# The head of a fused cross-attention and gated feed-forward kernel, issued in another order

## The chip, the cores and the metric

The kernel runs on one core of one Trainium2 chip. The metric is the device time of one execution in microseconds (us), the median of several runs; lower is better. A core has five engines with an instruction queue each: PE (TensorE, matrix products; its weight loads are shown as PEld), DVE (VectorE), ACT (ScalarE), POOL (GpSimd) and SP (SyncE, which issues DMA transfers). Each engine has its own list of instructions, in the order in which the program records them, and waits where one needs something that is not there yet.

## The reference

Two stages. The first is an attention in both directions between x (8 batches, 8 heads, 512 rows, 64 wide) and a state (8 batches, 8 heads, 32 rows, 64 wide):

```python
scores = scale * np.matmul(x, state.transpose(0, 1, 3, 2))
a = softmax(scores)                       # over the 32 state rows
xread = np.matmul(a, state)
scores2 = scale * np.matmul(state, x.transpose(0, 1, 3, 2))
a2 = softmax(scores2)                     # over the 512 rows of x
sread = np.matmul(a2, x)
y = np.concatenate([xread, sread], axis=2)    # 8 batches of 544 rows
```

The second puts the heads side by side, which gives 4352 tokens of width 512, and runs a gated feed-forward with 1536 inner channels over them:

```python
gate = 1.0 / (1.0 + np.exp(-(y @ w_gate)))
val = y @ w_val
out = (gate * val) @ w_out
```

## The kernel before, in words

**Stages of one batch b.** x of the batch is brought to bf16 and transposed (xT); S_mm multiplies it with the state, spread out so that two heads share one product (sTd for batches 0 and 1, sTz for the later ones); S_exp is the exponential; n_sum and n_mul divide by the row sums and give ab; aT is ab transposed. The state is multiplied with the two weight matrices ahead of time: sw_visit and sw_wide put state x (w_gate, w_val) into PSUM tiles named swp, and sw_cp copies them to SBUF as SW in bf16. gv_mm(b, f) is then the gate and value product of 128 of the 1536 channels, four matmuls of 128x512: both factors are ready, so xread itself is never formed. gv_th is the tanh on ACT (a sigmoid in other clothes), gv_glu the product of gate and value on DVE, which frees the value bank. The output product of a batch is done by seven half-size products in Strassen's manner (h_mm(k, c) for batch 0, c being the half of the rows); it needs sums of glu (h_sum, tile Sm) and sums of w_out (ht_sum, tile tw from tile wo). rd_mm and rd_fin make sread.

**Order.** There is no scheduler: the program is recorded as it is written. The first part of the body, called the head here (275 calls, lines 562 to 837), is a list written out call by call, in which batches 0 and 1, the weights and the start of batch 2 are interleaved. Behind it, step(b, f) runs for b = 2 to 8 and f = 0 to 11 with rules of its own; the first thing that step(2, 0) issues on PE is the swp tiles of batch 3 (sw_six, lines 286 and 293).

**PSUM.** Eight pools of one bank each are named G0, G1, OU, S0, S1, S2, S3 and AT. Every product names its bank or banks, so a product waits until whoever reads the bank's last content is done with it. The bank names in the list are therefore part of the order.

**Transfers.** x of batch 0 comes in four parts through SP (load_xp, line 87). What is cast to bf16 on the way, or loaded while SP is taken, goes through the queue of POOL: x of batch 1 in two halves (load_xh, line 100), the two weight matrices in slices of 256 or 512 channels (load_w, line 104), later states (load_sb, line 527), x of batch 2 (load_x, line 82), and w_out in three thirds (load_wo, line 107). An issue takes POOL 0.74 to 0.92 us. The framework hands out eight semaphores in turn to the transfers of this queue, so the issue of a transfer also waits until the transfer eight places ahead of it has landed. at_xT_dma (line 140) and aT_dma (line 248) are transposing transfers, issued by SP.

**Other lines that the steps name.** 95: the cast of x of batch 0; 135: copy of xT out of PSUM; 147, 156 and 174: S_mm in its forms; 186 and 188: sum and reciprocal of a quarter (nq_sum); 193: nq_mul; 208, 210 and 227: n_sum and n_mul; 234 and 244: aT and its copy; 265 and 268: rd_mm; 329: sw_cp; 343 and 355: gate/value products, in the head and in step; 364: gv_th; 369: gv_glu; 400: ht_sum; 407: h_sum; 425 and 442: output products; 433: w_add and U4; 517: warm, a product of zeros that no one reads; 540 and 543: the state's transposes; 551: sT_pad.

Of the kernel before, what the change touches and what calls it, by code (L numbers as in the profile page):

```python
# [16 lines left out]
def kernel(  # L17
# [310 lines left out]
    def sw_cp(b, lo, w, e, cp):  # L328
        cp(*sw_left.pop((b, lo, w, e)))  # L329
# [387 lines left out]
    load_wo(1)
    sw_cp(0, 512, 1, 0, vec)
    rd_mm(1, S2)
    sw_cp(1, 512, 0, 1, act)  # L720
    gv_mm(0, 5, G1, OU)
    rd_fin(1)
    gv_th(0, 5)
    gv_mm(0, 7, S1, S3)
    sw_cp(1, 512, 1, 0, vec)
    sw_cp(1, 512, 1, 1, act)
    gv_glu(0, 5)
    nc.gpsimd.memset(xs[:, :, :, D:], 1.0)
    gv_mm(0, 4, S0, G0)
    gv_th(0, 7)  # L730
    gv_glu(0, 7)
    gv_th(0, 4)
    gv_glu(0, 4)
    gv_mm(0, 6, S1, G1)
    cast_x(2, pool, 4, 4)
    load_wo(2)
    gv_th(0, 6)
    sw_wide(2, 1, S3, OU, S0, G0, S2, AT)
    gv_glu(0, 6)
    sw_cp(2, 1, 0, 1, act)  # L740
    sw_cp(2, 1, 0, 0, vec)
    sw_cp(2, 1, 1, 1, vec)
    sw_cp(2, 1, 1, 0, act)
    gv_mm(1, 5, S1, G1)
    gv_th(1, 5)
    gv_glu(1, 5)
    sw_cp(2, 1, 2, 0, act)
    h_sum(0, 1, vec)
    gv_mm(1, 6, OU, S3)
    sw_visit(1, 1280, 256, S1, G0)  # L750
    gv_th(1, 6)
    sw_cp(2, 1, 2, 1, act)
    sw_visit(1, 0, 256, S2, S0)
# [283 lines left out]
```

## Time and profile before

| | |
|---|---|
| median of 3 runs | 213.46 us (213.04 to 213.48) |
| the profiled execution | 213.24 us |
| its span, first to last instruction | 211.5 us |
| mean granted TensorE clock | 0.992 |
| busy: PE, DVE, ACT, POOL | 204.5, 160.7, 129.6, 78.7 us |
| HBM read, written | 18.35 MB, 8.91 MB |

The profile is one execution. "Busy" is the time in which an engine has an instruction under way; rows of a timeline give the start, the time taken, the engine, the line, the operation, the output and input tiles with their shapes, and a count where several follow each other. In brackets stands how long the engine stood idle ahead of it, and whom it waited for. A row that covers several instructions includes the tail of the last, which the start of the next may overlap. A row of the DMA view gives the size of a transfer and the time from issue to landing. All times count from the first instruction of the span.

### The profile page before, as it was taken

The page shows a single profiled execution, that of the slowest core. Times are in us where ns is not written, and L with a number is a line of the kernel's source. Part 1 is how long each engine was busy: PE and PEld are TensorE (multiplying, and loading weights), DVE is VectorE, ACT ScalarE, POOL GpSimd, SP SyncE. Part 2 cuts the span into 40 slices and gives each one's busy share as a digit, 9 for nine tenths or more (in the row PEclk, how much of TensorE's full clock was granted, in tenths as well). Part 3 has the DMA queues.
Part 4 walks back from the last instruction along what each step waited for, and adds up shares of the span by engine and source line. Part 5 has one row for each costly group of instructions (what it writes and reads, how often), then busy time and mean ns, then how long its engine had stood idle before and what let it go on. Part 6 is the DMA issues. An engine that isn't in the chain of part 4 may idle for free.

```text
span 211.5 us, 5331 instructions
## 1 busy us (share of the span) xinstructions
PE 204.5 (97%) x2089; PEld 133.4 (63%) x2089; DVE 160.7 (76%) x308; ACT 129.6 (61%) x244; POOL 78.7 (37%) x104
## 2 busy tenths in 40 slices
PE   7789999999999999999999999999999999999992
PEld 2555443677666666565656565657566666788982
DVE  2698899998987788578876887687848876864682
ACT  3878898754767477855786578647774673233210
POOL 8899467599042705900391029301500000000010
PEclk9799999999999999999999999999999999999999
DMA  6999999761689943985924621264110500130044
GB/s 190 181 192 192 213 289 192 115 215 38 78 219 342 132 94 133 289 73 160 295 58 48 186 87 28 56 101 175 26 34 1 201 2 0 76 126 0 4 171 126
DMA packets 40920, 27.14 MB, mean 128 GB/s; under 512 B 23616, under 2 KB 38720, under 8 KB 40896
## 3 DMA queue, kind: packets, MB, share of 16 engines
q1 hardware_dynamic: 30544, 19.47, 36.9%
q0 software_dynamic: 9920, 7.01, 20.5%
q10 hardware_dynamic: 432, 0.33, 0.7%
q8 instruction: 16, 0.26, 0.5%
q14 instruction: 8, 0.07, 0.1%
HBM read 18.35 MB, written 8.91 MB: 129 GB/s over the span
## 4 chain that ended last, share of the span: by engine, by line
PE 94%; DMA 2%; DVE 1%; ACT 1%; SPq 0%; issue 0%
PE gvp L355 30%; PE outp L425 29%; PE gvp L343 10%; PE gvp L358 5%; PE outp L442 4%; PE swp L286 4%; PE swp L293 2%; PE outp L484 2%; DMA xf<-in_x_dram 2%; PE Sp L147 1%; PE xTp L132 1%; PE outp L467 1%; PE rdp L262 1%; PE warm L517 1%; PE aTp L234 1%; PE rdp L265 1%
## 5 line engine op out<-in xcount | busy, mean ns | idle before, releaser
L369 DVE SCALAR_TENSOR_TENSOR glu<-th,gvp 128x512 bf16<-128x512 f32 (+1 forms) x108 | 70.1, 654 | 36.7 <-PE gvp L355 13.7
L364 ACT ACTIVATE th<-gvp 128x512 f32<-128x512 f32 (+1 forms) x108 | 62.1, 578 | 49.4 <-PE gvp L355 34.8
L355 PE MATMUL gvp<-aT,SW 128*128 128x512 bf16 x288 | 77.5, 380 | 0.1
L329 ACT CAST SW<-swp 128x512 bf16<-128x512 f32 x83 | 46.6, 594 | 9.2 <-PE swp L286 8.3
L425 PEld LDWEIGHTS <-Sm 128*128 128x128 bf16 x324 | 31.7, 98 | 12.6
L355 PEld LDWEIGHTS <-SW 128*128 128x128 bf16 x288 | 26.6, 98 | 17.3 <-issue 3.6
L200 POOL CAST Eb<-E 128x256 bf16<-128x256 f32 x32 | 12.8, 436 | 52.0 <-ACT E L167 52.0
L425 PE MATMUL outp<-tw,Sm 128*128 128x256 bf16 x240 | 31.8, 273 | 0.0
L425 PEld LDWEIGHTS <-glu 128*128 128x128 bf16 x240 | 23.5, 98 | 10.2
L425 PE MATMUL outp<-wo,glu 128*128 128x256 bf16 x168 | 22.9, 273 | 0.0
L343 PE MATMUL gvp<-aT,SW 128*128 128x512 bf16 x96 | 22.6, 380 | 0.0
L509 POOL DMA_DIRECT2D out_dram<-res x1 | 0.6, 612 | 50.3 <-DVE res L433 50.3
L227 POOL TENSOR_TENSOR ab<-E,ri 128x512 bf16<-128x512 f32 x13 | 14.3, 1101 | 11.7 <-DVE ri L210 7.0
L407 DVE TENSOR_TENSOR Sm<-glu 128x768 bf16<-128x768 bf16 (+1 forms) x34 | 18.0, 535 | 0.0
L433 DVE SCALAR_TENSOR_TENSOR res<-outp,U 128x512 f32<-128x512 f32 x22 | 15.0, 685 | 1.2 <-PE outp L442 0.9
L343 PEld LDWEIGHTS <-SW 128*128 128x128 bf16 x96 | 8.7, 98 | 10.5 <-issue 1.9
L116 POOL CAST xb<-xf 128x1024 bf16<-128x1024 f32 x12 | 13.2, 1127 | 1.6 <-DMA xf<-in_x_dram 1.6
L167 ACT ACTIVATE E<-Sp 128x512 f32<-128x512 f32 x14 | 8.4, 599 | 7.1 <-PE Sp L147 5.7
L358 PE MATMUL gvp<-xb,wgv 128*128 128x256 bf16 x96 | 12.6, 273 | 0.0
L425 PE MATMUL outp<-wo,Sm 128*128 128x256 bf16 x84 | 11.5, 273 | 0.0
L358 PEld LDWEIGHTS <-wgv 128*128 128x128 bf16 x96 | 9.3, 98 | 1.4
L251 POOL CAST xs<-xf 128x1024 bf16<-128x1024 f32 x10 | 10.1, 1040 | 0.0
(106 smaller groups left out, 224.9 us busy)
## 6 DMA issues: line engine op xcount, KB each, us to landing
out_dram<-res SPq DMA_DIRECT2D x14, 512.0 KB, 3.2
xf<-in_x_dram SPq DMA_DIRECT2D x5, 1024.0 KB, 7.5
wo<-in_moe_w_out_dram POOLq DMA_DIRECT2D x3, 512.0 KB, 8.2
xf<-in_x_dram SPq DMA_DIRECT2D x4, 256.0 KB, 4.0
wgv<-in_moe_w_gate_dram POOLq DMA_DIRECT2D x4, 256.0 KB, 7.4
wgv<-in_moe_w_val_dram POOLq DMA_DIRECT2D x4, 256.0 KB, 8.8
xf<-in_x_dram POOLq DMA_DIRECT2D x1, 1024.0 KB, 9.2
xf<-in_x_dram POOLq DMA_DIRECT2D x2, 256.0 KB, 6.2
```

The lines of the kernel that those rows point to most:

```text
L116: cp(xbs[b].rearrange("p c h d -> p h c d")[:, lo:lo + n], (xhs if b in xhs else xfs)[b][:, lo:lo + n])
L200: nc.gpsimd.tensor_copy(Ebs[b][:, c], E1s[b][:, c])
L227: (nc.gpsimd if eng is pool else nc.vector).tensor_tensor(half(b, i, abs_), e1, ri.unsqueeze(len(ri.shape)).to_broadcast(e1.shape), ALU.mult)
L329: cp(*sw_left.pop((b, lo, w, e)))
L343: nc.tensor.matmul(ps, SWs[b][:, g, w, fs], aTs[b][:, :, g], start=(g == 0), stop=(g == 1))
L355: nc.tensor.matmul(ps, SWs[b][:, g, w, fs], aTs[b][:, :, g], start=(g == 0), stop=(g == 1))
L358: nc.tensor.matmul(ps, (wg, wv)[w][:, j, fs], held["XS"][:, j], start=(j == 0), stop=(j == 3))
L364: nc.scalar.activation(th, held["gv", b, f][0], AF.Tanh, scale=0.5)
L369: nc.vector.scalar_tensor_tensor(glus[b][:, f], held["th", b, f], 1.0, held["gv", b, f][1], ALU.add, ALU.mult)
L407: eng.tensor_tensor(S_(b, t)[:, i], a, c, op)
L425: nc.tensor.matmul(wps[key][:, c], lhs[:, i, c * 128:(c + 1) * 128], rhs[:, i], start=(first and c == 0 and i == 0), stop=(i == NF // 2 - ...
L433: nc.vector.scalar_tensor_tensor(to, wps[key], 0.5, held["w", name], ALU.mult, ALU.add)
```

## The change

All of it is in the head; what it computes stays as it was. Every call of the old list stands in the new one, at another place, many with another bank, some on another engine. The few lines below carry what the prediction speaks of; the rest of the list is moved in the same manner.

```diff
+    load_xp(0, nc.sync, 4, 2)
+    load_xp(0, nc.sync, 2, 2)
+    zero(sTd, vec)
     make_identity(nc, ident)
-    load_xh(1, 0, 4)
-    nc.vector.memset(ones, 1.0)
-    cast_s(0, vec)
     cast_xp(0, act, 0, 2)
     load_xh(1, 4, 4)
...
+    warm(3, S3)
     xT_mm(0, 1, S3)
...
-    warm(3, G0)
...
-    aT_cp(0, 0, act)
-    sw_cp(0, 256, 2, 0, vec)
+    aT_cp(0, 0, vec)
+    sw_cp(0, 256, 2, 0, act)
...
+    load_x(2, nc.gpsimd)
+    nc.gpsimd.memset(xs[:, :, :, D:], 1.0)
...
+    load_wo(2)
...
+    load_wo(0)
...
+    load_wo(1)
...
+    gv_glu(1, 6)
+    ht_sum(0, vec)
```

Two halves of x of batch 1 change places, the slices of the weights at channel 0 move ahead, and all three state loads (load_sb) now come behind the eight narrow weight transfers, where one of them came behind four. The thirds of w_out come in the order 2, 0, 1.

On ACT, at the first state x weight copies, before (E is S_exp's output; the quarters of batch 0 are the 128x8x32 ones):

```order
L182 ACTIVATE E_177<-Sp 128x8x32 x2
L135 COPY xT<-xTp 128x1024
L167 ACTIVATE E_265<-Sp 128x8x64
L244 COPY aT<-aTp 128x512 x2
L167 ACTIVATE E_265<-Sp 128x8x64
L329 CAST SW<-swp 128x2x256 x2
L364 ACTIVATE th<-gvp 128x512
L329 CAST SW<-swp 128x2x256 x4
```

and after:

```order
L182 ACTIVATE E_197<-Sp 128x8x32 x2
L167 ACTIVATE E_311<-Sp 128x8x64
L135 COPY xT<-xTp 128x1024
L167 ACTIVATE E_311<-Sp 128x8x64
L244 COPY aT<-aTp 128x512
L329 CAST SW<-swp 128x2x256 x4
L364 ACTIVATE th<-gvp 128x512
L329 CAST SW<-swp 128x2x256 x2
L364 ACTIVATE th<-gvp 128x512 x4
```

Half of the aT copy has gone to DVE, and four SW copies stand ahead of the first tanh where two did.

On POOL, from the last weight slice to the casts of x of batch 2, before (tw is the tile that the later states are loaded to, sTz and xs are filled with constants):

```order
L200 CAST Eb<-E_265 128x256 x4
L111 MEMSET sTz 128x2048
L82 DMA xf<-in_x_dram 128x8x256
L107 DMA wo<-in_moe_w_out_dram 128x4x512
L557 COPY sTz<-sTc 64x24x32 x2
L107 DMA wo<-in_moe_w_out_dram 128x4x512
L728 MEMSET xs 128x32x2
L116 CAST xb<-xf 128x4x4x64
L107 DMA wo<-in_moe_w_out_dram 128x4x512
L407 TENSOR_TENSOR Sm<-glu 128x768
L116 CAST xb<-xf 128x4x4x64
```

and after:

```order
L200 CAST Eb<-E_311 128x256 x4
L527 DMA tw<-in_state_dram 128x4x64
L111 MEMSET sTz 128x2048
L82 DMA xf<-in_x_dram 128x8x256
L710 MEMSET xs 128x32x2
L107 DMA wo<-in_moe_w_out_dram 128x4x512 x3
L116 CAST xb<-xf 128x4x4x64 x2
L407 TENSOR_TENSOR Sm<-glu 128x768
L557 COPY sTz<-sTc 64x24x32 x2
```

The three thirds of w_out are issued in one go, and both casts of x of batch 2 follow without anything between them.

On DVE, around the sums of w_out, before (glu are gv_glu's, rs and ri belong to n_sum of batch 2):

```order
L369 SCALAR_TENSOR_TENSOR glu<-th,gvp 128x512 x3
L400 TENSOR_TENSOR tw<-wo 128x1536 x2
L407 TENSOR_TENSOR Sm<-Sm,glu 128x768
L400 TENSOR_TENSOR tw<-wo,tw 128x1536
L369 SCALAR_TENSOR_TENSOR glu<-th,gvp 128x512
L208 TENSOR_REDUCE rs<-E_911 128x16
L210 RECIPROCAL ri<-rs 128x16
L407 TENSOR_TENSOR Sm<-glu,Sm 128x768
```

and after:

```order
L369 SCALAR_TENSOR_TENSOR glu<-th,gvp 128x512 x3
L400 TENSOR_TENSOR tw<-wo 128x1536
L407 TENSOR_TENSOR Sm<-glu 128x768 x2
L400 TENSOR_TENSOR tw<-wo,tw 128x1536
L400 TENSOR_TENSOR tw<-wo 128x1536
L369 SCALAR_TENSOR_TENSOR glu<-th,gvp 128x512
L208 TENSOR_REDUCE rs<-E_885 128x16
L210 RECIPROCAL ri<-rs 128x16
L433 SCALAR_TENSOR_TENSOR res<-outp,V_911 128x2x256
```

ht_sum(0) now follows gv_glu(1, 6) instead of gv_glu(1, 11), with five gv_glu of batch 1 still to come instead of three, and the two h_sum of the sum tile 2 stand behind it.

More of the change, by code (lines that the diff above doesn't have):

```diff
@@ L586 @@
-    sT_pad(1, act)
-    xT_cp(0, 2, act)
+    cast_xp(0, vec, 2, 2)
+    cast_s(0, act)
+    xT_mm(0, 0, S3)
+    cast_xp(0, act, 4, 2)
+    sT_mm(0, S0)
+    nc.vector.memset(ones, 1.0)
+    xT_cp(0, 0, act)
+    load_xh(1, 0, 4)
+    sT_pad(1, vec)
+    sT_pad(0, act)
+    xT_mm(0, 2, G1)
+    load_w(0, 256, 256)
+    xT_cp(0, 2, vec)
+    load_w(1, 256, 256)
+    warm(3, S3)
+    xT_mm(0, 1, S3)
+    nc.scalar.activation(pre[:, 0:1], ones, AF.Exp)
+    load_w(0, 1024, 256)
+    xT_cp(0, 1, vec)
@@ L717 @@
[L717 to L753, printed above, removed]
+    xT_cp(1, 0, act, 2)
+    S_mm(1, 0, G0)
+    S_exp(1, 0)
+    aT_mm(0, S2)
+    aT_cp(0, 0, vec)
+    sw_visit(0, 256, 256, S3, S1)
@@ new lines @@
+    sw_cp(1, 512, 1, 1, vec)
+    rd_mm(1, G0)
+    gv_mm(0, 6, G1, OU)
+    load_wo(2)
+    sw_cp(1, 512, 0, 0, vec)
+    gv_th(0, 6)
+    gv_mm(0, 5, S2, AT)
+    rd_fin(1)
+    sw_cp(1, 512, 0, 1, act)
+    gv_mm(0, 7, G1, S0)
+    gv_th(0, 5)
+    gv_th(0, 7)
+    gv_mm(0, 4, G0, S2)
+    gv_glu(0, 6)
+    gv_glu(0, 5)
+    gv_th(0, 4)
+    load_wo(0)
+    sw_wide(2, 1, S3, S1, AT, G1, G0, OU)
+    gv_glu(0, 7)
+    load_wo(1)
+    sw_cp(2, 1, 1, 0, act)
+    sw_cp(2, 1, 1, 1, act)
+    cast_x(2, pool, 0, 4)
@@ new lines @@
+    sw_cp(2, 1, 0, 1, act)
+    sT_mm(3, S0)
+    gv_glu(0, 4)
+    sw_cp(2, 1, 2, 0, vec)
+    gv_mm(1, 5, S2, AT)
+    gv_th(1, 5)
+    gv_mm(1, 4, G1, G0)
+    sw_cp(2, 1, 0, 0, vec)
+    sT_cp(3, vec)
+    gv_th(1, 4)
+    gv_glu(1, 5)
+    gv_glu(1, 4)
+    cast_x(2, pool, 4, 4)
+    gv_mm(1, 6, S3, S0)
+    gv_th(1, 6)
+    sw_visit(1, 0, 256, G1, AT)
+    h_sum(0, 0, pool)
+    sw_cp(2, 1, 2, 1, act)
+    gv_glu(1, 6)
+    ht_sum(0, vec)
+    sw_visit(1, 1280, 256, S2, S1)
+    h_sum(2, 0, vec)
@@ L769 @@
-    gv_th(1, 11)
-    at_xT_dma(2)
-    gv_mm(1, 10, G0, S1)
-    gv_glu(1, 11)
-    h_mm(1, 0, AT)
-    h_mm(1, 1)
-    ht_sum(0, vec)
-    h_sum(0, 0, pool)
+    S_mm(2, 0, G1)
+    h_mm(1, 0, OU)
+    sw_cp(1, 0, 2, 1, act)
+    ht_sum(2, vec)
+    h_mm(1, 1)
+    gv_mm(1, 10, S0, S1)
+    gv_th(1, 10)
+    h_sum(1, 0, pool)
+    h_mm(2, 0, S3)
+    gv_glu(1, 7)
+    S_mm(2, 1, AT)
+    S_exp(2, 0)
+    h_mm(2, 1)
+    load_x(3, nc.sync)
+    gv_mm(1, 11, G1, G0)
+    gv_mm(1, 0, S2, S0)
+    n_sum(2, 0)
@@ L777 @@
+    w_keep('V1', 1)
+    S_exp(2, 1)
+    gv_th(1, 11)
+    gv_th(1, 0)
+    w_add(2, 'V1', w_res(0, 0)[:, :, lo_])
+    n_sum(2, 1)
+    gv_glu(1, 11)
+    h_sum(1, 1, pool)
+    gv_mm(1, 1, AT, S3)
+    gv_glu(1, 0)
+    n_mul(2, 0, pool)
+    gv_glu(1, 10)
+    h_mm(6, 0)
     h_mm(5, 0, G1)
-    S_mm(2, 0, OU)
     h_mm(5, 1)
-    ht_sum(2, vec)
-    h_sum(1, 0, vec)
-    load_x(3, nc.sync)
-    ht_sum(1, vec)
-    gv_th(1, 10)
-    h_mm(7, 0, S0)
-    gv_glu(1, 10)
-    sw_cp(1, 0, 2, 0, act)
@@ L788 @@
-    h_sum(3, 0, pool)
-    w_keep('V1', 1)
-    h_mm(6, 0)
-    S_exp(2, 0)
-    n_sum(2, 0)
-    n_mul(2, 0, pool)
-    S_mm(2, 1, G0)
-    aT_dma(2, 0)
-    S_exp(2, 1)
-    gv_mm(1, 0, OU, S2)
-    h_sum(3, 1, vec)
-    gv_th(1, 0)
-    h_mm(6, 1)
+    h_mm(6, 1)
+    h_mm(7, 0, S0)
+    gv_th(1, 1)
+    h_sum(3, 0, vec)
+    h_mm(7, 1)
     w_keep('U2', 1)
-    n_sum(2, 1)
+    cast_x(3, pool, 4, 4)
     ht_sum(3, vec)
     n_mul(2, 1, pool)
-    aT_dma(2, 1)
-    h_U4()
-    gv_mm(1, 1, G0, S1)
```

258 lines of the change are left out of this document (115 added, 143 removed).

## The prediction, made before the changed kernel ran

> **What bounds the kernel now.** I read the page first: the engine totals, the 40 slices and the chain that ended last.
>
> ```profile
> PE 204.5 (97%) x2089; PEld 133.4 (63%) x2089; DVE 160.7 (76%) x308; ACT 129.6 (61%) x244; POOL 78.7 (37%) x104
> PE   7789999999999999999999999999999999999992
> PEclk9799999999999999999999999999999999999999
> PE 94%; DMA 2%; DVE 1%; ACT 1%; SPq 0%; issue 0%
> ```
>
> TensorE is busy for 97% of the span and carries 94% of the last chain. Only the first three slices (5.29 us each) and the very last have PE under nine tenths. The change touches only the head, the code ahead of step(2, 0); all later work is PE-bound in the same order, so whatever the head wins or loses reaches the end of the span whole. I therefore ask one thing: when does PE issue the first row of step(2, 0)? The timeline of PE has that row, the first gate/value product, and what PE waited for ahead of it.
>
> ```profile
> 13.14 0.41 PE L293 MATMUL swp<-wgv,tw 64*32 64x512 bf16 x8 [0.20 <-DMA wgv<-in_moe_w_val_dram]
> 14.77 1.04 PE L343 MATMUL gvp<-aT,SW 128*128 128x512 bf16 x4
> 39.80 1.47 PE L442 MATMUL outp<-wo,glu 128*128 128x256 bf16 x12
> 52.77 0.62 PE L286 MATMUL swp<-wgv,sTc 64*32 64x512 bf16 x16
> ```
>
> The head ends at 52.77. The first product starts at 14.77, behind swp tiles that waited for a transfer of w_val. The timeline of POOL and the DMA view of that stretch say when it landed: 5.09 + 7.9 = 13.0.
>
> ```profile
> 5.09 0.76 POOL L104 DMA_DIRECT2D wgv<-in_moe_w_val_dram  x1
> wgv<-in_moe_w_val_dram POOLq DMA_DIRECT2D x1, 256.0 KB, 7.9
> ```
>
> **First part of the change: up to the first product.** The multiset of instructions in the head is the same (11 warm-up matmuls, 24 gate/value pairs, 14 groups of h_mm and so on); a few copies change engines and everything changes place. The two cast transfers that gate the first swp are still third and fourth on the pool's queue, behind the two halves of x of batch 1, so 13.0 stays. What PE has done before gv_mm(0, 3) is the same set before and after. What changes is who delivers ab, aT and SW for it, and these rows price that.
>
> ```profile
> 6.17 0.68 DVE L95 CAST xf<-xf 128x512 bf16<-128x512 f32 x1 [0.81 <-DMA xf<-in_x_dram]
> 6.76 0.41 DVE L135 COPY xT<-xTp 128x512 bf16<-128x512 bf16 x1
> 10.22 0.42 DVE L186 TENSOR_REDUCE rsq<-E 128x8 f32<-128x256 f32 x1
> 10.68 0.20 DVE L188 RECIPROCAL riq<-rsq 128x8 f32<-128x8 f32 x1
> 10.91 0.96 DVE L193 TENSOR_TENSOR ab<-E,riq 128x256 bf16<-128x256 f32 x2
> 12.57 0.69 DVE L208 TENSOR_REDUCE rs<-E 128x16 f32<-128x512 f32 x1
> 13.29 0.25 DVE L210 RECIPROCAL ri<-rs 128x16 f32<-128x16 f32 x1
> 13.61 0.69 DVE L329 CAST SW<-swp 128x512 bf16<-128x512 f32 x1
> 15.90 2.05 ACT L329 CAST SW<-swp 128x512 bf16<-128x512 f32 x4
> ```
>
> After, DVE runs in one piece from the landing of the third part of x at 6.17: cast 0.68, sT_pad (no row on DVE; between the narrow copy's 0.41 and the 0.69 of an f32 bank, L329; I take 0.6), two xT copies 0.82, a second cast 0.68, four sums with reciprocals 2.48, a wide xT copy (at most two narrow ones, I take 0.7), two products 0.96. That is 6.9, and ends at 13.1 with every tail counted, 12.7 where a start overlaps the tail before it; before, it was 10.91 + 0.96 = 11.87. Then a sum with reciprocal (0.94) and the aT copy (0.41) stand ahead on DVE, and ACT takes its aT half and both SW copies of batch 0 one behind the other (2.05 / 4 = 0.51 each), where before DVE did one of them. So aT is whole at about 14.2, the second SW copy ends at 15.2 (bounds 14.8 and 15.6), and the second matmul of gv_mm(0, 3) runs then, where it ran at 14.77 + 0.22 = 15.0. I take +0.3 for the first product, from 0 to +0.6.
>
> **Second part: from there to h_mm(1, 0).** These are the unit prices of PE, from the chain of waits in order of time.
>
> ```profile
> 17.02 3.45 PE gvp L343 x16
> 33.20 0.56 PE swp L286 x16
> 46.74 3.28 PE outp L442 x30
> ```
>
> A gvp matmul is 0.216, a group of eight swp 0.28, an outp matmul 0.109. Before h_mm(1, 0) the old order had run 22 of the 24 gate/value pairs; the new one has run 20, and one S_mm (0.23) more. So PE gets to h_mm(1, 0) at 39.80 - 2 x 0.86 + 0.23 = 38.3, plus the 0.3 above, less what the order wins back of the old stalls. Those are at most 0.8: 14.77 to 52.77 is 38.0, and 96 gvp (20.7), 84 outp (9.2), 128 swp (4.5) and some 2.8 of small products make 37.2. I take 0.3 of it, so 38.3, from 37.8 to 38.6. DVE gets to ht_sum(0), which reads all of wo, when glu(1, 6) is done: PE's gv_mm(1, 6) ends 1.65 (two swp groups of eight, one pair, S_mm) ahead of h_mm(1, 0), th and glu follow with 0.6 each, so at 37.9.
>
> Both need the last third of wo. Here are the issues on POOL and, from the DMA view of those stretches, the times to landing.
>
> ```profile
> 21.70 0.92 POOL L82 DMA_DIRECT2D xf<-in_x_dram  x1
> 22.59 0.78 POOL L107 DMA_DIRECT2D wo<-in_moe_w_out_dram  x1
> 28.38 0.75 POOL L107 DMA_DIRECT2D wo<-in_moe_w_out_dram  x1
> 31.93 0.74 POOL L107 DMA_DIRECT2D wo<-in_moe_w_out_dram  x1
> xf<-in_x_dram POOLq DMA_DIRECT2D x1, 1024.0 KB, 9.2
> wo<-in_moe_w_out_dram POOLq DMA_DIRECT2D x1, 512.0 KB, 10.6
> wo<-in_moe_w_out_dram POOLq DMA_DIRECT2D x1, 512.0 KB, 8.2
> wo<-in_moe_w_out_dram POOLq DMA_DIRECT2D x1, 512.0 KB, 7.0
> ```
>
> x of batch 2 landed at 30.9, the thirds of wo at 33.2, 36.6 and 38.9: one queue that hands over a third every 2.3 to 3.4 us however early it was issued. The last stood 0.9 ahead of its first use at 39.80. After, the bytes ahead of x are the same, the third state load included, and POOL issues all of it early (x at about 23, the thirds by 26), so nothing there holds the queue. The last third lands between 30.9 + 3 x 2.3 = 37.8 and 38.9; I take 38.35. It is now wanted at 37.9 by DVE and 38.3 by PE, so this wait binds, just. It also absorbs the 0.3 of the first part. Queued behind it on DVE are two h_sum, two ht_sum and glu(1, 7), whose bank gv_mm(1, 11) needs.
>
> at_xT_dma(2) moves up too; its four transposes on SP started at 35.99, 1.3 apart. With x cast in one go on POOL (2 x 1.03 behind 30.9) they start at 33.0 and S_mm(2, 0) needs the second at about 37: hidden, by a microsecond. load_x(3) follows them on SP at about 38, in the tail of the last third; that price has no row and lies in the bounds above. The third state load stands ahead of x, so it is in by 30.9, and sT_mm(3) comes 4.5 of PE work ahead of h_mm(1, 0), at 33.8: nothing. The tightest weight is the wide half of w_val:
>
> ```profile
> 17.85 0.79 POOL L104 DMA_DIRECT2D wgv<-in_moe_w_val_dram  x1
> wgv<-in_moe_w_val_dram POOLq DMA_DIRECT2D x1, 512.0 KB, 10.1
> ```
>
> It landed at 27.95, no later after (the same bytes but one state load ahead), and is wanted 9.95 of PE work ahead of h_mm(1, 0), at 28.35: hidden by 0.4, which I count at nothing; without it the loss is that of the wait for wo, which comes later on the same queue.
>
> **Third part: from wo to the end of the head.** DVE's work up to h_sum(3, 1), for which the fourth matmul of h_mm(3, 0) waits, has these rows.
>
> ```profile
> 39.99 1.82 DVE L400 TENSOR_TENSOR tw<-wo 128x1536 bf16<-128x1536 bf16 x2
> 35.85 1.02 DVE L407 TENSOR_TENSOR Sm<-glu 128x768 bf16<-128x768 bf16 x2
> 38.19 1.88 DVE L369 SCALAR_TENSOR_TENSOR glu<-th,gvp 128x512 bf16<-128x512 f32 x3
> 49.40 1.35 DVE L433 SCALAR_TENSOR_TENSOR res<-outp,U 128x512 f32<-128x512 f32 x2 [0.20 <-PE outp L442]
> ```
>
> Four ht_sum at 0.91, four h_sum at 0.51, five glu at 0.63, two n_sum at 0.94, U4 and one w_add at 0.68: 3.6 + 2.0 + 3.1 + 1.9 + 1.4 = 12.0 with tails, 11.4 where starts overlap tails. PE then has 21 outp (2.3) and rd_mm (0.6): 14.3 to 14.9 in all, I take 14.6. PE's own work behind the last third is 84 outp less the two that need it not, 4 pairs, an S_mm, sw_wide and rd_mm: 14.1, hidden behind the DVE chain. The head ends at 38.35 + 14.6 = 52.95 instead of 52.77: **+0.2**. The profiled execution took 213.24, so 213.44 for one like it; it is 0.22 below the median of the runs, 213.46, and against that I forecast 213.7. This kernel's measurement can tell about 0.2% (0.43 us) from no change.
>
> **The rivals.** *A, faster (0.20):* the queue gives wo at 2.3 us a third, or earlier, and the new order leaves PE no gaps. Then the last third is in at 37.8, the chain behind it is 14.3, the head ends at 52.1: -0.6, 212.9. For it: two of three distances in the rows are 2.3. Against: the middle one is 3.4, and DVE has no gap to give. [...]
>
> *B, slower (0.23):* ACT falls behind at the start, and PE's bank waits push the arrival at h_mm(1, 0) past 38.4, from where each 0.1 counts. The place is gv_mm(1, 8): its value half writes bank G0, in which th(1, 3) still reads the gate of gv_mm(1, 3), and th(1, 3) now stands behind the aT half, four SW copies, th(0, 3) and two more SW copies: 13.6 + 0.5 + 2.05 + 0.6 + 1.0 + 0.6 = 18.4, against PE's arrival at 19.1. With ACT late by more than the 0.7 between, PE stops there and again at each later reuse; I price that at 1.0 in all (two times th's 0.6, less the 0.2 to spare): 214.5.
>
> *C, slower (0.10):* the clock closes late. Three windows of the first stretch, with PE's busy time and, third from the end, the granted clock:
>
> ```profile
> 6.00:7.00 1.00, 0.10 (x2) 0.10 (x3) 0.83 (x2) 0.98 (x2) 1.00 (x2) 1.00 1.20 184
> 7.00:8.00 1.00, 0.73 (x17) 0.60 (x17) 0.59 (x2) 0.89 (x4) 1.00 (x2) 0.94 1.18 149
> 8.00:9.00 1.00, 1.00 (x13) 0.83 (x11) 0.84 (x3) 0.71 (x3) 0.78 (x2) 0.50 1.30 160
> ```
>
> The mean over the span, from the view of the cores:
>
> ```profile
> core 0: 211.5 us, clock 0.992
> ```
>
> The clock fell in the window from 7 to 8 and stood at 0.50 in the next, right behind a microsecond in which PE was busy for a tenth. The new order puts warm(3) into that gap, so I expect the clock open there. But from 11 to 15 PE now waits for ab, aT and SW. If it idles there as long as it did from 6 to 7, the clock falls again, just as the bound part begins. One such fall costs what the mean of 0.992 says: 0.008 x 211.5 = 1.7 us of clock, or 3.4 us at a half. Here it would hit products, and only 0.1 of waiting for wo absorbs it: 213.46 + 1.7 - 0.1 = 215.1. It decides at about 0.9 us of idle time in one piece; my walk has 0.3 to 0.5 in each of two. [...]
>
> **How the numbers follow.** Forecast 0.47 (faster 0.04, same 0.34, slower 0.09), A 0.20 (0.16 faster, 0.04 same), B 0.23 (0.07 same, 0.16 slower), C 0.10 slower: faster 0.20, same 0.45, slower 0.35. The range takes A's end, 213.46 - 0.65 = 212.8, and on the other side the late bounds together (38.9 + 14.9 = 53.8, +1.0) with some of B: 214.7. C and the tails of A and B stay out.
>
> **What would show it.** Right: ht_sum(0) on DVE waits for a DMA of wo for up to 1 us near 38; PE's h_mm(3, 0) waits for DVE; the row at 52.77 comes within 0.5 of it; the first gvp starts at 14.8 to 15.3. A: DVE waits for nothing at ht_sum(0) and the row comes at 52.1. B: ACT's th rows of batch 1 end after PE asks for their banks between 18 and 24. C: a granted clock under 1 behind 14.7. The forecast is wrong if wo lands before 37.5, or if the row at the end of the head has moved by over 0.7 without a wait for wo.

## The result and the profile after

| | before | after |
|---|---|---|
| median (range) | 213.29 us (213.04 to 213.48, 4 runs) | 220.23 us (218.27, 219.18, 221.28, 221.44) |
| mean granted clock of these runs | 0.992 (the profiled one) | 0.999, 0.992, 0.977, 0.975, in that order |
| profiled execution, its span | 213.24, 211.5 | 218.27, 216.5 |
| head ends (first L286 row of step(2, 0)) | 52.77 | 57.86 |

The changed kernel is slower: the ratio is 1.0317, with an interval of 1.0226 to 1.0408. The forecast was 213.7 with a range to 214.7. Left out here and below is one later execution of the changed kernel, in which the clock stood at 0.85 throughout, and out of the ratios single runs over 1.5% above the fastest of their kernel. Two things have to be explained: 5 us in the best run, which had the clock open throughout, and 3.2 us between the runs.

On the page of the changed kernel, PE's total, its 40 slices, its granted clock and the chain that ended last:

```profile
PE 205.2 (95%) x2089; PEld 132.5 (61%) x2089; DVE 164.6 (76%) x309; ACT 128.9 (60%) x243; POOL 79.8 (37%) x104
...
PE   7779999859999999999999999999999999999993
...
PEclk9999999999999999999999999999999999999999
...
PE 73%; DVE 9%; DMA 8%; POOL 5%; issue 2%; ACT 0%; SPq 0%; DVEq 0%; POOLq 0%
```

PE is as busy in all as before (205.2 against 204.5), but the eighth and ninth slices, 38 to 49 us, stand at 8 and 5 tenths, and DVE and POOL now carry part of the last chain, where PE had 94% of it. The clock is open in every slice: warm(3) stands in the gap in which it had closed, and in this run it did not close later either.

The timeline of PE has the places that the prediction named:

```profile
15.16 1.31 PE L343 MATMUL gvp<-aT,SW 128*128 128x512 bf16 x4 [1.03 <-ACT SW L329]
39.60 0.29 PE L147 MATMUL Sp<-sTz,xT 128*128 128x64 bf16 x4 [0.58 <-DMA xT<-xb]
40.10 0.29 PE L147 MATMUL Sp<-sTz,xT 128*128 128x64 bf16 x4 [0.21 <-DMA xT<-xb]
40.23 1.47 PE L442 MATMUL outp<-wo,glu 128*128 128x256 bf16 x12
46.84 2.32 PE L343 MATMUL gvp<-aT,SW 128*128 128x512 bf16 x10 [2.30 <-DVE glu L369]
57.86 0.63 PE L286 MATMUL swp<-wgv,sTc 64*32 64x512 bf16 x16
```

The first product starts at 15.16, 0.4 later than before (forecast 0.3). S_mm(2, 0), forecast as hidden, waits for both of its transposes, and h_mm(1, 0) starts at 40.23 instead of 38.35. A wait of 2.30 follows, in which the value half of gv_mm(1, 11) wants a bank that glu(1, 7) has not read yet. From h_mm(1, 0) to the end of the head pass 17.63 us; the forecast had 14.6. The two differences, 1.88 and 3.03, are nearly the whole 5.09 by which the head ends later than before (57.86 against 52.77); the forecast itself had 0.2.

Why glu(1, 7) is late stands on DVE's timeline:

```profile
39.39 1.23 DVE L400 TENSOR_TENSOR tw<-wo 128x1536 bf16<-128x1536 bf16 x1 [0.98 <-DMA wo<-in_moe_w_out_dram]
40.55 3.90 DVE L407 TENSOR_TENSOR Sm<-glu 128x768 bf16<-128x768 bf16 x2
46.11 0.67 DVE L369 SCALAR_TENSOR_TENSOR glu<-th,gvp 128x512 bf16<-128x512 f32 x1
50.81 0.55 DVE L407 TENSOR_TENSOR Sm<-glu,Sm 128x768 bf16<-128x768 bf16 x1
51.28 1.79 DVE L400 TENSOR_TENSOR tw<-wo,tw 128x1536 bf16<-128x1536 bf16 x1
```

The two h_sum at 40.55 take 1.95 each, where the row of before has 0.51. At 50.81 the same operation takes 0.55, and at 51.28 an ht_sum takes 1.79 instead of 0.91. Nothing in the rows waits; the instructions themselves are long. The timeline of POOL at the same places:

```profile
38.18 1.63 POOL L407 TENSOR_TENSOR Sm<-glu 128x768 bf16<-128x768 bf16 x1
39.77 4.26 POOL L407 TENSOR_TENSOR Sm<-Sm,glu 128x768 bf16<-128x768 bf16 x2
50.88 1.37 POOL L116 CAST xb<-xf 128x1024 bf16<-128x1024 f32 x1
52.20 2.16 POOL L200 CAST Eb<-E 128x256 bf16<-128x256 f32 x4
54.31 2.36 POOL L251 CAST xs<-xf 128x1024 bf16<-128x1024 f32 x2
```

POOL does h_sum(1, 0) and (1, 1) at 39.77, in 4.26 (one alone 1.63, the row at 38.18), and a cast beside the long ht_sum. In the old list h_sum(1, 0) was on DVE, and (1, 1) on POOL at another time.

### The profile page after: what moved, and what is told of

Same layout as the page of the kernel before. It is cut to its first block, busy times and chain, and to the rows that moved or that the text cites. A ratio compares the mean times of both kernels' runs of the same rounds, so it can differ in the third digit from the quotient of the medians.

```text
span 216.5 us, 5323 instructions
## 1 busy us (share of the span) xinstructions
PE 205.2 (95%) x2089; PEld 132.5 (61%) x2089; DVE 164.6 (76%) x309; ACT 128.9 (60%) x243; POOL 79.8 (37%) x104
## 4 chain that ended last, share of the span: by engine, by line
PE 73%; DVE 9%; DMA 8%; POOL 5%; issue 2%; ACT 0%; SPq 0%; DVEq 0%; POOLq 0%
PE gvp L355 29%; PE outp L425 28%; DMA wo<-in_moe_w_out_dram 6%; PE gvp L358 5%; PE swp L286 3%; DVE tw L400 2%; PE outp L484 2%; DMA xf<-in_x_dram 2%; DVE glu L369 2%; PE outp L442 1%; POOL wgv L104 1%; DVE Sm L407 1%; PE swp L293 1%; PE Sp L147 1%; PE outp L467 1%
## 5 line engine op out<-in xcount | busy, mean ns | idle before, releaser
L369 DVE SCALAR_TENSOR_TENSOR glu<-th,gvp 128x512 bf16<-128x512 f32 (+1 forms) x108 | 69.6, 653 | 35.7 <-PE gvp L355 13.8
L425 PEld LDWEIGHTS <-Sm 128*128 128x128 bf16 x324 | 31.7, 98 | 12.6
L200 POOL CAST Eb<-E 128x256 bf16<-128x256 f32 x32 | 13.7, 465 | 53.4 <-ACT E L167 53.4
L407 DVE TENSOR_TENSOR Sm<-glu 128x768 bf16<-128x768 bf16 (+1 forms) x34 | 20.9, 618 | 0.0
L227 POOL TENSOR_TENSOR ab<-E,ri 128x512 bf16<-128x512 f32 x13 | 13.6, 1049 | 15.8 <-DVE ri L210 7.4
L343 PEld LDWEIGHTS <-SW 128*128 128x128 bf16 x96 | 8.8, 97 | 14.6 <-issue 4.1
L358 PE MATMUL gvp<-xb,wgv 128*128 128x256 bf16 x96 | 12.6, 273 | 0.0
```

Source lines behind the costliest of these rows:

```text
L200: nc.gpsimd.tensor_copy(Ebs[b][:, c], E1s[b][:, c])
L227: (nc.gpsimd if eng is pool else nc.vector).tensor_tensor(half(b, i, abs_), e1, ri.unsqueeze(len(ri.shape)).to_broadcast(e1.shape), ALU.mult)
L343: nc.tensor.matmul(ps, SWs[b][:, g, w, fs], aTs[b][:, :, g], start=(g == 0), stop=(g == 1))
L358: nc.tensor.matmul(ps, (wg, wv)[w][:, j, fs], held["XS"][:, j], start=(j == 0), stop=(j == 3))
L369: nc.vector.scalar_tensor_tensor(glus[b][:, f], held["th", b, f], 1.0, held["gv", b, f][1], ALU.add, ALU.mult)
L407: eng.tensor_tensor(S_(b, t)[:, i], a, c, op)
```

## The experiments

Times are of one execution, the fastest, with the clock open where nothing else is said; the kernel before took 212.9 in such runs on every chip used (its lowest runs there are 212.92, 212.86, 212.72 and 212.89). Theory P: DVE's sums, which read two tiles of SBUF, stand still while POOL executes an instruction that reads SBUF, and the other way round. Theory M: those rows are long for a reason of their own (the tiles, the memory traffic). Theory K: the rest comes from falls of the clock. Theory Q: the cast queue, with x of batch 2 ahead, sets when wo and the transposes are in.

**1. The sums taken off POOL, a reading and a writing load in their place.**

```diff
 e1, e2, e3:
-    h_sum(1, 0, pool)
+    h_sum(1, 0, vec)
-    h_sum(1, 1, pool)
+    h_sum(1, 1, vec)
 e2 adds on POOL at both places (no one reads scr):
+    nc.gpsimd.tensor_tensor(scr, S_(0, 0)[:, i], A(0, 0, 0)[:, i], ALU.subtract)
 e3 adds instead, three times at each place:
+    nc.gpsimd.memset(scr, 0.0)
```

Both sums on DVE:

> The changed kernel, with h_sum(1, 0) and h_sum(1, 1) on DVE instead of POOL. Theory P (DVE's sums of two SBUF tiles wait while POOL reads SBUF): the two h_sum of tile 2 on DVE, which took 1.99 us each beside POOL's sums, take 0.5 each; the two moved ones add 0.5 each; the head ends at 57.86 - 2.9 + 1.0 = 55.9 or a little under, and a run at full clock takes 216.3 instead of 218.3. Rival M (DVE's sums are slow because x of batch 3 is landing at over 300 GB/s at that time): all sums on DVE in that stretch stay near 2.0, the head ends at 58 or later, 218.5 or more.

With sums on POOL that no one needs (scr is a part of the tile tw that is free at that time):

> As the one with the sums on DVE, and POOL does two sums of the same tiles and size at the old place, into a tile that nobody reads. Theory P: DVE's sums in that stretch wait for POOL again (1.5 to 2.0 us for at least two of them), the head ends at 57.9 to 58.9, a run at full clock takes 218.3 to 219.3. Rival M: POOL's work changes nothing, the result is that of the kernel without it.

With memsets on POOL:

> As before, but POOL fills the unread tile six times (about 0.7 us each) instead of summing: it is as long busy, and only writes. Theory P in the form that only POOL's reads count: no loss against the kernel with the sums on DVE, head end 55.9, 216.3 at full clock. Rival P2 (any POOL instruction blocks DVE there): DVE's sums of 1 to 2 us, 217.3 or more. Rival M: as without it.

Measured: 217.06, 219.99 (lowest, clock 0.992) and 217.26; ratios 1.022 (1.0136 to 1.0304), 1.0347 (1.0262 to 1.0431) and 1.0195 (1.0121 to 1.0269). The profile of the third is one of its longer runs (220.84), whose clock stood at a half from 11.0 to 21.2; the rows below lie behind that. Here are DVE's row for h_sum(2, 0) and (2, 1) in the three, and what POOL did beside it. The sums on DVE, POOL idle beside the first row:

```profile
40.40 1.01 DVE L407 TENSOR_TENSOR Sm<-glu 128x768 bf16<-128x768 bf16 x2
48.83 1.18 DVE L407 TENSOR_TENSOR Sm<-glu,Sm 128x768 bf16<-128x768 bf16 x1
52.20 1.22 DVE L407 TENSOR_TENSOR Sm<-glu,Sm 128x768 bf16<-128x768 bf16 x1
```

POOL reading:

```profile
41.06 3.90 DVE L407 TENSOR_TENSOR Sm<-glu 128x768 bf16<-128x768 bf16 x2
40.28 4.26 POOL L567 TENSOR_TENSOR tw<-Sm,glu 128x768 bf16<-128x768 bf16 x2
```

POOL writing only:

```profile
44.03 1.01 DVE L407 TENSOR_TENSOR Sm<-glu 128x768 bf16<-128x768 bf16 x2
43.23 4.72 POOL L567 MEMSET tw<- 128x768 bf16 x6
```

The same two instructions on the same tiles take 1.01, 3.90 and 1.01. POOL is busy for over four microseconds in both of the last two; only where it reads does DVE stand. P holds and M falls, by these three rows. In e1 the late sums (48.83, 52.20) are still long, since POOL casts beside them, and so it takes 217.06 where 216.3 was forecast.

**2. The clock behind the wait of 2.30.**

```diff
+    warm(8, S2)
     gv_mm(1, 11, G1, G0)
```

> The changed kernel with eight more warm-up products (8 x 0.216 = 1.73 us at full clock) ahead of gv_mm(1, 11), where PE waits 2.9 us in two pieces. Theory K (the spread from 218.3 to 221.4 and the mean clocks from 0.999 to 0.975 come from a clock that falls behind this wait in some runs): all runs within 1 us of 218.3, mean clock 0.99 or more. Rival: the clock falls elsewhere, and the runs spread by 2 to 3 us as they did, with clocks down to 0.975.

Measured: 218.36, 218.38, 219.53 and 221.17, ratio 1.0265 (1.0189 to 1.034). The spread stays, and the best run is no better than the changed kernel's. The profiled run, the longest, lost its time earlier: its clock stands at a half from 13.7 to 20.6. The run of 219.53 has a mean clock of 0.998, so not all of the spread is the clock's. The fall that lengthens the runs is thus not, or not only, behind that wait. It can be there: with POOL reading, PE waited 3.18 ahead of the same product, and the ten gvp behind it took 4.00 instead of 2.32.

**3. POOL's casts given to ACT, and PE's order.**

```diff
 e4, on top of the sums on DVE:
-    cast_x(3, pool, 4, 4)
+    cast_x(3, act, 4, 4)
-    cast_x(3, pool, 0, 4)
+    cast_x(3, act, 0, 4)
-    at_Eb(2)
+    for c in range(4): act(Ebs[2][:, c], E1s[2][:, c])
 cast_xs(3, ...) stands behind step(2, 1)
 e5, on top of e4:
-    S_mm(2, 0, G1)
     h_mm(1, 0, OU)
...
     h_mm(1, 1)
+    S_mm(2, 0, G1)
...
-    h_mm(6, 0)
     h_mm(5, 0, G1)
     h_mm(5, 1)
+    h_mm(6, 0)
```

> Both sums of the run before this one stay on DVE, and POOL is kept from reading SBUF until the head ends: the two casts of x of batch 3 and the casts to Eb go to ACT, the casts to xs move behind step(2, 1). If POOL's reads are what slows DVE's sums, h_sum(3,0), ht_sum(3) and h_sum(3,1) take 0.5, 0.9 and 0.5 us (1.18, 1.15 and 1.22 with the two sums alone moved), DVE is done with h_sum(3,1) at about 51.8 instead of 53.4, the wait of 0.66 on PE ahead of the fourth matmul of h_mm(3,0) goes, and since PE then has no later DVE work to wait for, the head ends at 55.9 instead of 56.5 and the best run takes 216.4 (217.06 there). If those rows were long for a reason of their own (tile, place in PSUM, the clock), they stay over 1.1 and the best run stays at 217.1. ACT gets some 3 us of casts; if it has no such room, sw_wide's copies come late and the time rises above 217.1.

> As the run with POOL kept silent, and two products move on PE: S_mm(2,0) stands behind h_mm(1,1), so that nothing ahead of h_mm(1,0) needs the transposes of x of batch 2, and both halves of h_mm(5) stand ahead of h_mm(6,0), so that it finds h_sum(1,1) done. If the transposes' landing is a cost of its own, h_mm(1,0) starts when the last third of wo is in, at 39.1 instead of 39.9, and with the wait of 0.85 for Sm gone as well the head ends 1.6 earlier than with POOL silent alone, at about 54.2: 214.8 for the best run. If PE is held by wo and by DVE in any case, the wait moves to h_mm(1,0) and the head gains 0.3 at most: 216.1.

Measured: best runs 217.90 and 217.61, ratios 1.0257 (1.0189 to 1.0324) and 1.0233 (1.0167 to 1.0298). The first forecast of 216.4 failed because the edit did not do what it says: POOL waits for nothing at its place in the list, so the casts to xs ran at once, at 47.66, beside the sums. POOL and DVE of that kernel:

```profile
46.67 1.05 POOL L227 TENSOR_TENSOR ab<-E,ri 128x512 bf16<-128x512 f32 x1 [0.35 <-DVE ri L210]
47.66 2.35 POOL L251 CAST xs<-xf 128x1024 bf16<-128x1024 f32 x2
```

```profile
46.98 1.15 DVE L407 TENSOR_TENSOR Sm<-Sm,glu 128x768 bf16<-128x768 bf16 x1
49.25 1.17 DVE L407 TENSOR_TENSOR Sm<-glu,Sm 128x768 bf16<-128x768 bf16 x1
50.35 0.94 DVE L400 TENSOR_TENSOR tw<-wo,tw 128x1536 bf16<-128x1536 bf16 x1
52.41 0.54 DVE L407 TENSOR_TENSOR Sm<-glu,Sm 128x768 bf16<-128x768 bf16 x1
```

Where POOL reads beside them, h_sum(1, 1) and h_sum(3, 0) are long; behind POOL's last cast, ht_sum(3) and h_sum(3, 1) are at their price. That is P again, row by row. The casts on ACT have a cost of their own: rd_mm waited 0.61 for SW copies. Without the wait for the transposes only 0.3 was gained, as the second reading said. In e5's profile PE waits 1.03 and 0.76 for glu instead, but that is a run of 220.00, whose clock had fallen at 12.1; which wait took over in the best run isn't shown.

**4. x of batch 2 on another queue.**

```diff
 e7, in the changed kernel (e8: the same on top of e5):
-    load_x(2, nc.gpsimd)
+    load_x(2, nc.scalar)
```

> The changed kernel with one edit: x of batch 2 is issued by ACT, on a queue that does not cast, at the same place in the list; the three thirds of wo then follow the weights directly on the cast queue. If that queue's own rate sets when wo is in (a third every 2.3 to 3.4 us behind 1 MB of x), wo lands 4 us earlier, at about 35, x no later than 31, ht_sum(0) starts when glu(1,6) is done, at 38.2 instead of 39.4, S_mm(2,0) does not wait, and the best run takes 217.2 (218.27 with x on the cast queue), since the slow sums beside POOL stay. If the 16 engines or the memory set it, wo lands within 1 us of 39 and the time stays at 218.3.

> POOL silent, the two products moved and x of batch 2 on ACT's queue together. If the costs are the slow sums beside POOL, the wait for the transposes and the wait for wo, in that order, then h_mm(1,0) starts at 38.9 and the head ends at about 54.0: 214.6 for the best run, and what is left above 213.0 (the kernel before) is the late arrival of PE, 38.9 against 38.3 by my walk, and the stretch behind it. If something else holds the head back, the best run stays above 216.

Measured: 223.31 and 223.25 at best, at clocks of 0.981 and 0.985 (no run of the eight has it open), ratios 1.0479 (1.0426 to 1.0532) and 1.0506 (1.0434 to 1.0578). ACT reached the issue only at 29.06, 6 us later than POOL did, and the casts and pad of POOL queued behind the landing at 39.0, so that S_mm(2, 0) waited 7.42 for POOL in e7. The clock fell in it and stood at a half from 44.4 to 51.2, so not all of the loss is the wait. As a test of Q it is half a test: with x out of the way, ht_sum(0) found wo there at 38.41, and the last third had landed at 36.6 (24.3 + 12.3), against 39.1 in the changed kernel (25.2 + 13.9). The better test came with the next group.

**5. POOL really held, the other queue again, and warm-up products.**

```diff
 e9: h_sum(1, 0) and (1, 1) on vec, the second behind gv_glu(1, 7), and:
     h_sum(3, 1, vec)
+    pool(pre[:, 1:2], Sm[:, 3, 5, :1])
+    at_Eb(2)
+    cast_x(3, pool, 4, 4)
+    cast_x(3, pool, 0, 4)
 e11: e9, and load_x(2, nc.scalar) behind gv_th(0, 9)
 e10: the changed kernel, and e12: e11, each with
+    warm(2, G0)
     Sq_mm(0, 0, S0)
...
+    warm(2, G0)
     S_mm(1, 1, S3)
...
+    warm(3, G1)
     gv_mm(0, 3, S3, G1)
```

> Both sums of batch 0 on DVE, the second of them now right behind glu(1,7), and POOL held by a copy of one column of h_sum(3,1)'s result: its casts to Eb, of x of batch 3 and to xs all come behind that. (The run called POOL silent did not silence it: the casts to xs ran ahead, beside h_sum(3,0).) If POOL's reads make DVE's sums long, h_sum(1,1), h_sum(3,0), ht_sum(3) and h_sum(3,1) take 0.55, 0.55, 0.95 and 0.55 us, h_sum(3,1) ends at about 51.6 instead of 53.4, PE waits for no Sm, the head ends at 55.0 (56.5 with the two sums alone moved) and the best run takes 215.6 (217.06 there). If DVE's rows shrink and the end stays, another wait takes over, and the rows of PE name it; if they don't shrink, POOL was not the cause.

> As the run with POOL held, and x of batch 2 goes on ACT's queue, issued behind th(0,9), at about 20.5 (29.1 in the run before that tried this queue, where it landed at 39.0, because ACT got there late). If the cast queue's rate sets when wo is in, wo lands at 35 to 36, x at about 31, ht_sum(0) starts at 38.2, h_mm(1,0) at about 39.0, and the best run takes 0.9 less than with POOL held alone: 214.7. If x lands after 33 on this queue too, POOL's casts and pad come late, and the time does not fall.

> The changed kernel with seven more warm-up products, in the three longest gaps of PE before the first gate/value product: two ahead of the first quarter of S, two ahead of S_mm(1,1), three ahead of gv_mm(0,3). The runs of the changed kernel lie between 218.27 (mean clock 0.999) and 221.44 (0.975), and in two disturbed profiles the clock fell at 10.9 and 13.6 for three and two windows of 3.4 us. If idle PE in these gaps lets the clock fall, all runs now show a mean clock of 0.99 or more and lie within 0.6 of the best, which stays at 218.3 (to 218.6, if the products end after the wait they stand in). If the falls come from elsewhere, the spread of 3 us stays.

> The run with POOL held and x of batch 2 on ACT's queue, with the seven warm-up products as well: the best run as without them (214.7 if both theories hold), all runs within 0.6 of it, so a median of 214.9, against 213.0 for the kernel before. What is then left above it, 1.7 to 1.9, is DVE's chain from ht_sum(0) on with two sums more on it, and the arrival of PE at 38.9.

Measured, POOL held: 216.66 to 217.48, ratio 1.0178 (1.0144 to 1.0213). Its DVE rows and PE:

```profile
39.04 1.36 DVE L400 TENSOR_TENSOR tw<-wo 128x1536 bf16<-128x1536 bf16 x1 [0.86 <-DMA wo<-in_moe_w_out_dram]
48.56 0.55 DVE L407 TENSOR_TENSOR Sm<-glu,Sm 128x768 bf16<-128x768 bf16 x1
49.03 0.95 DVE L400 TENSOR_TENSOR tw<-wo,tw 128x1536 bf16<-128x1536 bf16 x1
51.10 0.55 DVE L407 TENSOR_TENSOR Sm<-glu,Sm 128x768 bf16<-128x768 bf16 x1
55.26 1.37 DVE L407 TENSOR_TENSOR Sm<-glu 128x768 bf16<-128x768 bf16 x1
56.66 1.27 DVE L407 TENSOR_TENSOR Sm<-Sm,glu 128x768 bf16<-128x768 bf16 x1
```

```profile
39.33 0.29 PE L147 MATMUL Sp<-sTz,xT 128*128 128x64 bf16 x4 [0.54 <-DMA xT<-xb]
39.94 1.47 PE L442 MATMUL outp<-wo,glu 128*128 128x256 bf16 x12
54.74 0.62 PE L286 MATMUL swp<-wgv,sTc 64*32 64x512 bf16 x16
59.05 1.02 PE L355 MATMUL gvp<-aT,SW 128*128 128x512 bf16 x4 [0.77 <-DVE glu L369]
```

Behind ht_sum(0), which POOL's h_sum(0, 1) still holds up (1.36), all sums of the head are at their price, no row of PE names a wait for one, and the head ends at 54.74 (forecast 55.0). DVE's chain, from wo at 39.04 to the end of h_sum(3, 1) at 51.65, takes 12.6 with two sums more on it; the prediction's 12.0 and 1.0 for these make 13.0. PE takes 14.80 from h_mm(1, 0) to the end of the head without a named wait, so here its own work sets the pace at least as much as DVE does; the prediction had put that work, less two outp, at 14.1, hidden behind DVE. But the run won only 1.6 of the 3.12: the held casts to xs now run beside the sums of step(2, 0) (1.37 and 1.27 on DVE), and PE waits there, 0.77 at 59.05.

x on ACT's queue, issued at 21.87 this time: 218.12 to 218.44, ratio 1.0246 (1.021 to 1.0283), 1.5 slower than without. In that kernel POOL's first cast and DVE's ht_sum(0) show the landings:

```profile
33.65 2.02 POOL L116 CAST xb<-xf 128x1024 bf16<-128x1024 f32 x2 [8.73 <-DMA xf<-in_x_dram]
39.22 2.23 DVE L400 TENSOR_TENSOR tw<-wo 128x1536 bf16<-128x1536 bf16 x1 [0.95 <-DMA wo<-in_moe_w_out_dram]
```

x landed at 33.6, 11.7 after its issue, and wo no earlier (39.04 with x on the cast queue). Q falls in the form in which I had it: wo does not come earlier when x is taken off its queue but travels beside it; in e7, where x was issued behind the thirds, it did. That points to something that both queues use. The 16 DMA engines, over nine tenths busy in every slice from 20 to 36 us in the changed kernel and in e11, are the likely one; that is argued, not tried. Of the 1.5, 1.05 lie in the head, which ends at 55.79, and a good part of that is P once more: POOL's casts, pad and h_sum(0, 1) come later behind x, and ht_sum(0) beside the last takes 2.23, against 1.36.

The warm-up products in the changed kernel gave 218.29, 218.35, 220.08 and 220.55, ratio 1.029 (1.0232 to 1.0349); on top of e11, 217.67 to 218.38, ratio 1.0229 (1.0196 to 1.0262). In the profiled one of 220.55 PE waited 3.35 for glu(1, 7) and the ten gvp behind it took 3.70: a late fall. None of the eight shows a clock under 0.992, but neither did those of e9 and e11 on that chip, so this did not settle the early falls.

**6. The casts to xs on ACT, the order, and the clock once more.**

```diff
 e13: e9, with cast_xs(3, ...) on ACT, behind gv_th(1, 0) and w_keep('U2', 1)
 e14: e13, with S_mm(2, 0), h_mm(5) and h_mm(6) as in e5, and
-    h_sum(1, 0, vec)
...
     gv_glu(1, 7)
+    h_sum(1, 0, vec)
 e15: e13, with the warm-up products of e10
 a0: the changed kernel
```

> The changed kernel as it is, beside the three others on one chip. If its spread is a matter of falls of the clock, the time goes with the mean clock: 218.3 at 0.999, about 1 us more for each 0.008 below that (one window of 3.4 us at a half), up to 221.4; its median 218.3 to 220.3, depending on how many runs fall.

> As the run with POOL held, and the two casts to xs go to ACT, into its gaps at about 46 and 50, so that POOL is done when step(2, 0) begins its sums at 55.3. If those casts beside the sums are what gave back 1.5 us, the sums there take 0.55 each (1.37 and 1.27), PE's waits of 0.77 and 0.45 for glu go, and the best run takes 215.2 (216.66 with POOL held alone), with the head's end still at 54.7. If ACT has no room, th(1,1) comes late and gv_mm waits for its bank: 216 or more. With falls of the clock in the first stretch as in the changed kernel, single runs lie 1 to 3 us above the best.

> As the run with the casts to xs on ACT, with S_mm(2,0) behind h_mm(1,1), h_mm(5) ahead of h_mm(6,0), and glu(1,7) ahead of h_sum(1,0) on DVE. If the wait for the transposes (0.54 and 0.20 on PE) is worth its length now that DVE is no longer late, h_mm(1,0) starts at 39.2 and the head ends at 54.1: 214.6 for the best run. If DVE is the bound all the same, or the wait for wo takes over, the gain is under 0.2: 215.1.

> As the run with the casts to xs on ACT, with the seven warm-up products in the gaps of the first stretch. If idle PE there makes the clock fall, all runs show a mean clock of 0.995 or more and lie within 0.6 of the best (215.2 to 215.4), while the same kernel without them shows falls in some of its runs, as the changed kernel does. If both show the same spread, the falls come from elsewhere or the products don't count; if neither shows falls but the changed kernel does, the late wait of 2.3 us is what makes them.

Measured:

| | us, with the mean clock | ratio |
|---|---|---|
| a0 | 218.13 (1.000), 218.77 (1.000), 218.78 (0.999), 219.91 (0.992), 221.12 (0.984) | 1.0292 (1.0251 to 1.0334) |
| e13 | 215.28 (1.000), 215.57 (0.997), 215.68 (0.996), 215.84 (1.000), 218.74 (0.984) | 1.0113 (1.0087 to 1.0139) |
| e14 | 215.37 (1.000), 215.54 (0.999), 217.66 (0.984), 218.58 (0.984) | 1.0173 (1.012 to 1.0225) |
| e15 | 215.43 to 217.81, six runs, all 0.997 or more | 1.0152 (1.0115 to 1.0189) |

The longer times of a0 go with the clock, at 1.5 to 1.8 us for each 0.008 rather than the 1 of the forecast (219.91 at 0.992, 221.12 at 0.984); the two runs of 218.8 lie 0.6 above the best at the same clock. e13 came out at 215.28 for a forecast of 215.2: with the casts away from the sums of step(2, 0), these are at their price, and 1.4 of the 1.5 lost behind the head is back.

```profile
58.32 0.55 DVE L407 TENSOR_TENSOR Sm<-glu 128x768 bf16<-128x768 bf16 x1
```

Keeping POOL's reads off DVE's sums is thus worth 2.9 of the 5.2 (218.13 to 215.28), with two sums moved to DVE and two casts to ACT included. e14 gained nothing, as its second reading said. In its profile PE waits 0.56 for glu and 0.48 for DVE's bank, but the clock had fallen at 12.5 there, PE came later than the transposes anyway, and e13's profile is of that kind too; which wait binds in the best runs isn't shown.

The clock: the profiled run of e13 is the one of 218.74. Its windows, with PE's busy time first and the granted clock third from the end, and behind them the row of PE with the longest wait ahead of the fall:

```profile
11.00:13.00 2.00, 1.26 (x37) 0.82 (x37) 1.93 (x7) 1.50 (x2) 2.00 (x5) 1.00 1.45 195
13.00:15.00 2.00, 2.00 (x60) 1.35 (x60) 0.92 (x4) 0.60 (x2) 1.81 (x3) 0.71 1.44 195
15.00:17.00 2.00, 1.36 (x18) 0.23 (x3) 1.87 (x5) 2.00 (x5) 2.00 (x4) 0.50 1.47 203
17.00:20.00 3.00, 3.00 (x28) 1.37 (x27) 1.04 (x2) 1.49 (x4) 3.00 (x6) 0.50 1.44 182
```

```profile
12.39 0.21 PE L265 MATMUL rdp<-xf,Eb 128*32 128x64 bf16 x4 [0.41 <-POOL Eb L200]
```

The clock falls at about 13.8, less than a microsecond behind two in which PE was busy for 1.26, and stays at a half to past 20; 218.74 instead of 215.3. That is rival C, at the place that it named, and twice its length. Its condition was not met: PE was busy for six tenths of those two microseconds, and the longest idle piece ahead of the fall that its rows name is 0.41, less than half of the 0.9 at which the prediction, from the one fall in the profile of before, had it decide. Why the clock falls in one run of a list and not in another is not shown. Without the warm-up products, 5 of the 14 runs of this chip show a clock of 0.992 or less; with them, none of 6 (two of the four runs of e10 do, on another chip; the one that was profiled fell late, at 48.9). That fits idle PE in these gaps as the cause, and does not settle it: 0 of 6 is what 7 in 100 such sets would show by luck (9 of 14, to the sixth power), and e15's runs differ by 2.4 us at full clock, for another reason. In its profile the first part of x came 0.5 later than in the changed kernel's (ACT's first cast, at 4.49, waits 2.00 for it, against 1.47 at 3.95), and the first product at 16.83; what delays those transfers was not tried.

No version here beats the kernel before.

## Why the prediction was wrong

**The step that failed** is the third part: "Four ht_sum at 0.91, four h_sum at 0.51 ... 12.0 with tails". I took each price from a row of before in which POOL happened not to hold DVE up, and asked of every moved operation only what it waits for, not what runs beside it. The new list sets h_sum(1, 0) and (1, 1) on POOL right behind the landing of wo, just where DVE does its own sums. The chain took 15.4 (39.39 to 54.77) instead of 12.0. The sign stood in the profile of before, on the other engine: beside DVE's ht_sum POOL's own sum takes 2.29, and 1.64 where DVE does none.

```profile
42.19 0.95 DVE L400 TENSOR_TENSOR tw<-wo,tw 128x1536 bf16<-128x1536 bf16 x1
```

```profile
38.33 1.64 POOL L407 TENSOR_TENSOR Sm<-glu 128x768 bf16<-128x768 bf16 x1
42.35 2.29 POOL L407 TENSOR_TENSOR Sm<-glu,Sm 128x768 bf16<-128x768 bf16 x1 [2.39 <-DVE Sm L407]
```

Shown: the price of the pair with POOL idle, reading and writing (group 1), and the chain at about its forecast length with POOL held (group 5). P fits every row shown here. That DVE's order, not PE's, set the pace in the changed kernel is shown by the wait of 2.30 for glu(1, 7), which is gone in e9. A second term was short and stayed hidden behind the first: PE's own work behind h_mm(1, 0), put at 14.1, takes 14.80 in e9, as long as the whole chain of DVE was to take.

**"Hidden, by a microsecond"** (the transposes) was wrong by 3 us. x was cast at 31.41, and the transposes were issued at 33.46, by my walk 33.0. But they took long to land. From the view of the tile xT, first before, then after:

```profile
DMA to landing us min/median/max: 2.5/2.6/3.6
```

```profile
DMA to landing us min/median/max: 3.0/4.9/6.1
```

They now travel beside the thirds of wo. In e8, where they were issued from 40.4 on and wo was in by 35.5 (24.5 + 11.0), all four took 2.5, so that traffic is the likely cause; it was not tried by itself. The wait on PE is 0.58 and 0.21; taking it away was worth 0.3 at most.

**The last third of wo**: forecast 38.35, at most 38.9; it was in at 39.39, and ht_sum(0) waited 0.98 for it. The mechanism was right, the size 1.0 short. e7 and e11 show that it isn't x's place on the cast queue that sets it, but x travelling ahead of or beside the thirds (in at 36.6 with x issued behind them, at 39.2 with x beside them on ACT's queue); what the two queues share is left open.

**PE's arrival.** PE stood nowhere between its first product at 15.16 and the product ahead of S_mm(2, 0), which starts at 37.98 and ends, with four gvp of 0.216, at 38.84. By my walk it was there at 38.3 - 0.23 = 38.07. So PE came 0.8 later than I counted. The sum took 0.3 off for old stalls that the new order would win back, but the timeline of before names no wait of PE between 14.77 and 39.80 either: the 0.8 from which that was taken is a difference of unit prices, not idle time. Another 0.1 is the first product; which products make the rest I did not take apart.

**Right**: the first product (0.4 for 0.3); that PE has no slack behind the head (the span behind that point is 216.5 - 57.86 = 158.6 against 211.5 - 52.77 = 158.7, so the head's loss reached the end whole); that DVE waits for wo up to a microsecond. Rivals A and B did not occur: PE waits for nothing between 15.16 and 38.84. **Rival C**, given 0.10, did occur in runs, and not by its condition: the clock fell behind pieces of 0.41, and stayed open in the changed kernel's profile behind one of 1.03 (the row at 15.16). It was common: of the nine runs of the changed kernel listed here, five show a clock of 0.992 or less, and the median of the first four, 220.23, has 2 us of it over the open run. The profiled run alone does not show it; the list of the runs' clocks does.

What is left of the 5.2, 2.35 in e13: e9's head, with the same order, ended 1.8 behind the forecast, 1.6 of which lies ahead of h_mm(1, 0) (39.94 against 38.35): wo, the transposes and the arrival together. Without the wait for the transposes 0.3 (e5) and nothing (e14) was gained, with x on another queue something was lost, and PE's arrival was not tried.

## What to carry to other kernels

Where sums are moved between DVE and POOL, lay the two timelines side by side: a DVE operation with two inputs in SBUF and a POOL operation that reads SBUF cost about the sum of their times here (h_sum 0.51 on DVE and 1.63 on POOL alone, 1.95 and 2.13 side by side), so a price from a row in which the other engine was idle is a lower bound. To hold POOL back, its place in a list is not enough; it needs something to wait for (the casts to xs ran at 47.66 in e4, at 55.16 in e9, which holds POOL by a copy). And where the clock falls in some runs of one list and not in others, as in five of the nine runs of the changed kernel, a change is judged by the clocks of all its runs, not by one profile.
